# GpSimd's loads ahead of its scalings of v, and VectorE's order of work at the start of group 1, in a block attention with an MLP

## The chip, the cores and the metric

The kernel runs on one core of a Trainium2 chip. The metric is the device time of one execution in microseconds (us). Engines are named as the profile names them: PE is TensorE (PEld its weight loads), DVE is VectorE, ACT is ScalarE, POOL is GpSimd, SP is the queue that issues most stores and the DMA transposes.

## What is computed

Two stages follow each other. A linear attention with decay over blocks (4 batches, 8 heads, 768 positions, head size 64), then an MLP with an exact gelu on the 3072 tokens of 512 values:

```
for b in range(nb):
    intra = einsum('bhic,bhjc->bhij', qb, kb) * Dmask
    intra = einsum('bhij,bhjd->bhid', intra, vb)
    inter = einsum('bhid,bhde->bhie', qb * lam_pow, kv_state)
    out[:, :, sl] = intra + inter
    kv_state = lam_block * kv_state + einsum('bhsd,bhse->bhde', kb * rev_pow, vb)
x = out as (3072, 512);  h = x @ w_in (512 x 2048);  g = gelu(h);  result = g @ w_out (2048 x 512)
```

## The kernel before

**Tiling.** The work is cut into 24 chunks of 128 positions of one batch, and six groups of four chunks (M = 4, one chunk of each batch). Chunks 0 to 3 are group 0, chunks 4 to 7 group 1, chunks 8 to 11 group 2. The attention of one group's chunks is computed while the MLP of the group before runs on TensorE, so that TensorE always has matmuls. All work is in bfloat16 with sums in float32 in PSUM.

**A chunk.** Its k, q and v are loaded by GpSimd's DMA queue (`load`, L69 for the chunks touched here, L72 in halves for later ones), into 10 buffers for k and 8 each for q and v. v is scaled by powers of lambda (`decay_v`, L160, 128x512, on GpSimd; that of chunk 4 alone on VectorE). k and q are transposed on TensorE (L166) with the copies on ScalarE and VectorE (L169, L172), or from chunk 8 on by DMA transposes on SP (L181, L182). The scores are matmuls (L200), masked by VectorE (`masked`, L206: two operations a chunk, each out of one PSUM bank). The answers add what the states give (L248) and what the values give (L255); they are emptied into the group's x by ScalarE (L347), by VectorE for chunk 7 (L345). The states of the next group are made from products of k and scaled v (`next_products`, L215), an addition by VectorE (`added`, L234, called by `sums`) and a scaling by VectorE (`next_states`, L240, called by `new_states`).

**The MLP of a group.** Group 0 does the first product plainly (L666, with the gelu at L669). From group 1 on, part of the first product (L428) and the whole second product (L542) are done as seven products of half-sized blocks in place of eight. That takes sums of blocks: four sums of parts of w_in, once (`w_in_sums`, L389), four sums of x in each group (`x_sums`, L404), sums of w_out (L370) and of g (L521). The seven products gather in PSUM banks that ScalarE copies (L434) and VectorE adds up (`total`, L437). In the second product VectorE makes the last additions into the output tile (`upper`, L621; `lower`, L633) and SP stores it (L553). Of the seven first products of a group, the fifth needs the first sum of x and of w_in, the sixth the second ones, the third the fourth sum of w_in, the seventh the third ones, the fourth the fourth sum of x.

**The order.** It is written by hand: each engine does its instructions in the order in which the program issues them, and waits with semaphores for the others. The program walks over blocks of matmuls; before each block it issues what is due. In group 0 that is listed by block (`group0`, blocks counted from e = 19); from group 1 on a step is put at a place g + f, where B is the length of one plain block of 8 matmuls, so `1 + 4.5 * B` is four and a half blocks into group 1. The steps of group 1 that count here are `visit_at(1 + 1 * B, ...)`, which asks for the scores of chunks 6 and 7 and masks them, and `visit_at(1 + 4 * B, ...)`, which gives their answers and makes the products for the states. The sums of x are issued ahead of the blocks at 4 B (first two) and 4.5 B (last two). The scalings of v of chunks 8 to 11 come at 7 B, on GpSimd, behind a small copy that waits for the fourth sum of x (`behind_sums`, L889). PSUM has eight banks under the names sc, mh, mo (two each), t and o; the next user of a name waits until the last one is emptied.

**GpSimd's order around the change.** Loads of chunks 4 to 7, then for n = 5, 6, 7 the scaling of v of chunk n and the loads of chunk n + 3, then the loads of chunk 11. Each load takes GpSimd's time (L69), whether or not the data has landed.

Of the kernel before, what the change touches and what calls it, by code (L numbers as in the profile page):

```python
# [15 lines left out]
def kernel(  # L16
# [10 lines left out]
    nc = tc.nc  # L27

    B, H, S, D = q.shape
# [10 lines left out]
    M = 4  # L40
# [21 lines left out]
    def chunk_of(name, n):  # L62
        so, b = n // M, n % M
        return dram[name][b, :, so * C:(so + 1) * C, :].rearrange("h si d -> si h d")

    def load(n, name):
        raw[n, name] = qkv_pool.tile([128, H, D], BF16, tag=name, name=f"{name}_t", bufs=10 if name == "k" else 8)
        if name == "v" or n < N_UP:
            nc.gpsimd.dma_start(raw[n, name], chunk_of(name, n))  # L69
        else:  # L70
            for r in range(2):
                nc.gpsimd.dma_start(raw[n, name][:, r::2, :], chunk_of(name, n)[:, r * HP:(r + 1) * HP, :])  # L72
# [78 lines left out]
    def begin(n, early=False):  # L151
        c = Chunk()
        c.n, c.sb, c.early = n, n // M, early
        c.q, c.k, c.v = (raw.pop((n, name)) for name in "qkv")
        return c

    def decay_v(c, eng):

        c.v_dec = work_pool.tile([128, H, D], BF16, tag="vd", name="v_dec", bufs=6)
        eng.tensor_mul(c.v_dec, c.v, lam_m[:, :, None].to_broadcast((128, H, D)))  # L160
# [13 lines left out]
    def transposes(c, tags="mh mh"):  # L174
        for name, tag, empty in zip("kq", tags.split(), (nc.scalar.copy, scaled)):
            transposed(c, name, tag, empty)
# [205 lines left out]
    def w_in_sums(*which):  # L382
        lo, hi = (w_in_t[:, :, (k0 + KW[0]) * 128:(k0 + KW[0] + NW) * 128] for k0 in (0, KH))
        for i in which:
            w_in_s[i] = w_pool.tile([128, 2, NW * 128], BF16, name=f"wi_sum{i}")
            a, b, op = {1: lambda: (hi[:, :2], hi[:, 2:], ALU.add), 2: lambda: (w_in_s[1], lo[:, :2], ALU.subtract),
                        3: lambda: (lo[:, :2], hi[:, :2], ALU.subtract),
                        4: lambda: (lo[:, 2:], w_in_s[2], ALU.subtract)}[i]()
            nc.vector.tensor_tensor(w_in_s[i], a, b, op=op)  # L389
# [3 lines left out]
    def first_blocks(g, g_t, x_t, mm1):  # L393
# [105 lines left out]
        plan += [(his[2], plain), (y.p7, plain // 2), (his[3], plain), (y.p4, plain // 2)]  # L499
        return plan  # L500

    def blocks_by_seven(g, g_t, first):

        last = g == NG - 1
# [31 lines left out]
        banks, sb = {}, {}  # L536
# [13 lines left out]
        def store(rows, us, cols, queue=nc.sync):  # L550
            b = slice(rows * 2 + us.start, rows * 2 + us.stop)
            dst = out_r[g, :, b, cols]
            queue.dma_start(dst, sb[rows][:, us, cols])  # L553

        both, every = slice(0, 2), slice(0, d_model)

        def chain(i, name, u, begin=False):
            if begin and u == 0 and name == "a" and apart:
                banks["a"] = [bank([128, DH], F32, tag, "a_ps") for tag in ("mo", "t" if last else "mo")]
            elif begin and u == 0:  # L560
                all_us = bank([128, 2, DH], F32, "mo" if name == "a" else "mh", f"{name}_ps")
                banks[name], banks[name, "all"] = [all_us[:, 0, :], all_us[:, 1, :]], all_us
            product(i, u, banks[name][u], begin and (u == 0 or (apart and name == "a")))

        def per_bank(name, u, f):
            if (name, "all") not in banks:
                f(slice(u, u + 1), banks[name][u][:, None, :])
            elif u == 1:
                f(slice(0, 2), banks[name, "all"])
# [62 lines left out]
        def lower():  # L632
            nc.vector.tensor_add(sb[1][:, :, d_hi], sb["p5"], sb["u3"])  # L633

        def m4(u):
            chain(4, "a", u)
            per_bank("a", u, lambda us, a: nc.scalar.copy(sb[1][:, us, d_lo], a))
            if last:
                store(1, slice(u, u + 1), d_lo, nc.scalar if u else nc.sync)
            elif u == 1:  # L640
                if g == 0:
                    lower()
                store(1, both, every)

        order = ((m1, 0), (m1, 1), (m2, 0), (m2, 1), (m5, 0), (m5, 1), (m6, 0), (m6, 1), (m3, 0), (m7, 0), (m7, 1), (m3, 1),
                 (m4, 0), (m4, 1))
        if g == 0:
            order = [(f, u) for f in (m1, m5, m2, m3, m6, m7, m4) for u in range(2)]
            run, cost = blocks[N1 - 2]
            blocks[N1 - 2] = (lambda: ([g_sum(i, 0) for i in (1, 2, 4, 3)], run())), cost  # L650
# [47 lines left out]
    live = {}  # L698
# [52 lines left out]
    for n in range(M, 2 * M):  # L751
        live[n] = begin(n)
        if n > M:
            decay_v(live[n], nc.gpsimd)
            for name in "kqv":
                load(n + M - 1, name)
    for name in "kqv":
        load(3 * M - 1, name)
    next_load[0] = 3 * M
# [15 lines left out]
    def triangles():  # L775
        for p in HALVES:
# [20 lines left out]
        e + 11: [lambda: visit([], [4]), lambda: masks(4)],  # L797
        e + 12: [lambda: scores_by_quarters(live[5], "t o"), lambda: masks(5), lambda: transposes(live[6])],
        e + 13: [lambda: visit([4, 5], []), lambda: empties(4, 5), lambda: transposes(live[7], "mo mh"),
                 lambda: w_in_sums(1, 2)],  # L800
    }

    todo = []
# [1 line left out]
    def at(when, run):  # L805
        todo.append((place(when), run))

    def begin_at(when, n):
        def run():
            live[n] = begin(n)  # L810
            dma_transposes(live[n])
        at(when, run)
# [3 lines left out]
    def visit(done, asked, banks="mo mo", states_of=(), kv_tags="mh mh"):  # L816
        done = [live[n] for n in done]
        if done:
            o_ps = [bank([128, HP, C], F32, tag, "o_ps") for tag in ("o", "t")]
            from_states(done, o_ps, 0)  # L820
        for n, tags in zip(asked, ("sc sc", banks)):
            scores_by_quarters(live[n], tags)
        if done:
            if not asked:
                apart = bank([128, HP, C], F32, "sc", "apart_ps")
                for p in HALVES[::-1]:
                    nc.tensor.matmul(apart[p, 0, :], idle[p, :D], idle[p, :C], start=True, stop=True,
                                     skip_group_check=True)
            from_states(done, o_ps, 1)
            for n, tag in zip(states_of, kv_tags.split()):  # L830
                totals[n] = next_products(n, tag)
            for c, c.o_ps in zip(done, o_ps):
                from_values(c)
        for n in asked:
            prefetch(n + M)
# [21 lines left out]
    def empties(*chunks):  # L857
        for n in chunks:
            empty_outputs(live[n])
# [14 lines left out]
    def visit_at(when, done, asked, *then, **how):  # L874
        at(when, lambda: visit(done, asked, **how))
        for step in then:
            w, run = when, step[0]
            if isinstance(run, float):
                w, step = run, step[1:]
            at(w, lambda step=step: step[0](*step[1:]))  # L880

    B = 2 * M * 2 * C / later
# [27 lines left out]
    for i, w in enumerate((-0.07, 0.0, 0.13)):  # L910
        begin_at(1 + w, 2 * M + i)
    at(1 + 7 * B, lambda: prefetch(3 * M))
    begin_at(1 + 7 * B, 2 * M + 3)
    visit_at(1 + 1 * B, [], [2 * M - 2, 2 * M - 1], (masks, 2 * M - 1, 2 * M - 2),
             (w_in_sums, 4, 3), banks="t o")
    visit_at(1 + 4 * B, [2 * M - 2, 2 * M - 1], [], (empties, 2 * M - 2, 2 * M - 1), (sums, M, M + 2),
             (1 + 4.5 * B, new_states, M), (1 + 4.5 * B, new_states, M + 2), states_of=(M, M + 2), kv_tags="sc sc")
    n = 2 * M
    steps((1 + 7 * B, behind_sums, 1), (1 + 7 * B, decays, *range(n, n + M)),
          (1 + 7 * B, prefetch, 3 * M + 1), (1 + 11 * B, prefetch, 3 * M + 2),  # L920
# [9 lines left out]
    for g in range(2, NG):  # L930
        n = (g + 1) * M
# [27 lines left out]
    for g in range(1, NG - 2):  # L959
        n = (g + 2) * M  # L960
# [48 lines left out]
```

## Time and profile before

| | us |
|---|---|
| median of 3 runs | 198.13 |
| lowest and highest run | 197.66, 198.58 |
| the profiled execution | 198.04 |
| its span, from first to last instruction | 196.0 |
| PE busy in it | 187.9 (96%) |
| DVE busy | 135.2 (69%) |
| POOL busy | 112.1 (57%) |
| ACT busy | 106.3 (54%) |
| granted TensorE clock | 1.0 of full speed all through |

The profile is of one execution. Its timeline gives for each entry the start in us from the span's beginning, the busy time, the engine, the line of the program, the operation, what it writes and reads, the count, and in brackets the engine's idle time just before with what ended it. Entries that follow each other closely on one line are merged (x2, x4). Neighbours on an engine can overlap a little, as instructions are pipelined; the distance from start to start tells more than the busy time. The chain that ended last is followed back from the last instruction, at each step to what released it. Group 0's MLP ends at about 49.6 us, group 1's first product lies between 49.6 and 67 us.

### The profile page before, as it was taken

How to read it: one execution, taken by the hardware profiler on the slowest of the kernel's cores; microseconds unless marked ns; L12 is line 12 of the kernel's file. 1: busy time of each engine (PE TensorE's matmuls, PEld its weight loads, DVE VectorE, ACT ScalarE, POOL GpSimd, SP SyncE). 2: the span in 40 equal slices, each digit the busy share in tenths (PEclk: the TensorE clock that was granted, in tenths of full speed). 3: DMA queues.
4: the chain of work that ended last, by engine and by line, in shares of the span. 5: the costliest groups of instructions: out<-in, count | busy, mean ns of one | idle time of the engine just before them, and what ended most of it. 6: DMA issues, size and time to landing. Idle time of an engine off the chain costs nothing.

```text
span 196.0 us, 6742 instructions
## 1 busy us (share of the span) xinstructions
PE 187.9 (96%) x2932; PEld 160.4 (82%) x2932; DVE 135.2 (69%) x231; ACT 106.3 (54%) x210; POOL 112.1 (57%) x141
## 2 busy tenths in 40 slices
PE   7699999998999999999999999999999999999992
PEld 3278776997878898888999888999888888888881
DVE  3744509997998699597797398687459693545830
ACT  4954566144548812659932279712379522589231
POOL 8999992699997599998099756980040000000000
PEclk9999999999999999999999999999999999999999
DMA  4999999999999999999979999999600000400005
GB/s 115 146 170 176 195 197 197 165 157 220 155 215 124 159 123 146 137 144 285 135 47 126 103 201 242 83 89 123 244 2 3 0 3 27 190 3 0 0 3 214
DMA packets 104781, 24.82 MB, mean 127 GB/s; under 512 B 93232, under 2 KB 101936, under 8 KB 104752
## 3 DMA queue, kind: packets, MB, share of 16 engines
q0 software_dynamic: 83120, 13.38, 108.9%
q1 hardware_dynamic: 21488, 10.89, 28.4%
q8 instruction: 23, 0.38, 0.8%
q10 hardware_dynamic: 144, 0.13, 0.2%
q14 instruction: 6, 0.05, 0.1%
HBM read 27.27 MB, written 6.29 MB: 171 GB/s over the span
## 4 chain that ended last, share of the span: by engine, by line
PE 85%; DVE 7%; DMA 3%; POOL 2%; issue 1%; ACT 0%; POOLq 0%; DVEq 0%
PE h_ps L666 24%; PE a_ps L542 19%; PE c_ps L542 11%; PE ha_ps L428 9%; PE b_ps L542 5%; PE hc_ps L428 5%; DMA q_t<-in_q_dram 3%; DVE sc_m L206 2%; PE hb_ps L428 2%; PE o_ps L314 2%; PE o_ps L255 1%; PE kv_ps L290 1%; PE o_ps L326 1%; PE t_ps L166 1%; PE idle_ps L707 1%; PE sc_ps L279 1%
## 5 line engine op out<-in xcount | busy, mean ns | idle before, releaser
L666 PE MATMUL h_ps<-x_t,w_in_t 128*128 128x256 bf16 (+3 forms) x480 | 55.7, 266 | 0.2 <-DVE x_t L345 0.2
L666 PEld LDWEIGHTS <-w_in_t 128*128 128x128 bf16 x480 | 41.7, 98 | 7.4 <-DVE x_t L345 0.5
L669 ACT ACTIVATE g_t<-h_ps 128x512 bf16<-128x512 f32 (+2 forms) x59 | 34.1, 578 | 23.6 <-PE h_ps L666 23.6
L542 PEld LDWEIGHTS <-g_sum 128*128 128x128 bf16 x456 | 38.3, 98 | 3.6
L542 PEld LDWEIGHTS <-g_t 128*128 128x128 bf16 x360 | 29.3, 98 | 2.7
L160 POOL TENSOR_TENSOR v_dec<-v_t,lam_m 128x512 bf16<-128x512 bf16 x23 | 24.0, 1065 | 10.1 <-PE a_ps L542 5.4
L69 POOL DMA_DIRECT2D v_t<-in_v_dram x24 | 22.0, 915 | 4.2 <-DMA w_out_t<-in_moe_w_out_dram 1.8
L542 PE MATMUL a_ps<-w_sum,g_sum 128*128 128x256 bf16 (+1 forms) x240 | 23.2, 251 | 0.0
L521 DVE TENSOR_TENSOR g_sum<-g_t 128x1024 bf16<-128x1024 bf16 x24 | 16.0, 699 | 9.6 <-ACT g_t L669 9.6
L72 POOL DMA_DIRECT2D k_t<-in_k_dram x24 | 18.5, 791 | 0.0
L72 POOL DMA_DIRECT2D q_t<-in_q_dram x24 | 18.3, 790 | 0.0
L428 PEld LDWEIGHTS <-wi_sum 128*128 128x128 bf16 x160 | 15.6, 97 | 2.5 <-issue 0.2
L574 ACT COPY f_u<-a_ps 128x256 f32<-128x256 f32 (+1 forms) x16 | 7.7, 479 | 17.7 <-PE a_ps L542 17.7
L333 DVE TENSOR_TENSOR x_t<-o_ps,lam_q 128x512 bf16<-128x512 f32 x16 | 10.3, 684 | 4.2 <-PE o_ps L314 4.2
L440 ACT ACTIVATE g_t<-h_p 128x512 bf16<-128x512 f32 x20 | 12.9, 644 | 0.4 <-DVE h_p L437 0.3
L428 PEld LDWEIGHTS <-w_in_t 128*128 128x128 bf16 x120 | 11.6, 98 | 1.8
L69 POOL DMA_DIRECT2D k_t<-in_k_dram x12 | 11.1, 925 | 2.3 <-DMA w_out_t<-in_moe_w_out_dram 2.1
L542 PE MATMUL c_ps<-w_out_t,g_sum 128*128 128x256 bf16 (+1 forms) x112 | 12.3, 257 | 0.0
L428 PE MATMUL ha_ps<-x_sum,wi_sum 128*128 128x256 bf16 x80 | 12.0, 272 | 0.0
L437 DVE TENSOR_TENSOR h_u<-h_u,hc_ps 128x512 f32<-128x512 f32 x10 | 6.8, 684 | 7.3 <-ACT h_u L434 5.3
L69 POOL DMA_DIRECT2D q_t<-in_q_dram x12 | 10.9, 906 | 1.4 <-DMA w_out_t<-in_moe_w_out_dram 1.4
L542 PE MATMUL c_ps<-w_sum,g_sum 128*128 128x256 bf16 (+1 forms) x104 | 11.7, 265 | 0.0
(109 smaller groups left out, 326.4 us busy)
## 6 DMA issues: line engine op xcount, KB each, us to landing
out_dram<-o_sb SPq DMA_DIRECT2D x11, 512.0 KB, 5.1
v_t<-in_v_dram POOLq DMA_DIRECT2D x24, 128.0 KB, 6.4
w_out_t<-in_moe_w_out_dram POOLq DMA_DIRECT2D x4, 512.0 KB, 8.7
w_in_t<-in_moe_w_in_dram POOLq DMA_DIRECT2D x7, 256.0 KB, 7.6
k_t<-in_k_dram POOLq DMA_DIRECT2D x12, 128.0 KB, 6.6
q_t<-in_q_dram POOLq DMA_DIRECT2D x12, 128.0 KB, 5.9
k_t<-in_k_dram POOLq DMA_DIRECT2D x24, 64.0 KB, 5.3
q_t<-in_q_dram POOLq DMA_DIRECT2D x24, 64.0 KB, 5.1
```

Of the source, the lines that this page charges most:

```text
L69: nc.gpsimd.dma_start(raw[n, name], chunk_of(name, n))
L72: nc.gpsimd.dma_start(raw[n, name][:, r::2, :], chunk_of(name, n)[:, r * HP:(r + 1) * HP, :])
L160: eng.tensor_mul(c.v_dec, c.v, lam_m[:, :, None].to_broadcast((128, H, D)))
L333: nc.vector.tensor_mul(x[:, :, :, HALVES[t]], pairs[n].o_ps[t], lam_q[:, :, None, HALVES[t]].to_broadcast((128, HP, 2, D)))
L428: nc.tensor.matmul(self.banks[b][:, k, :], left[i](q, self.kf + k), right[i](q), start=(tag is not None and k == 0 and q == 0), stop=(q == 1),
L437: nc.vector.tensor_add(self.sb[name], self.sb[name], self.banks[b])
L440: nc.scalar.activation(g_t[:, k0 + self.kf:k0 + self.kf + 2, cols], src, ACT.Gelu)
L521: nc.vector.tensor_tensor(gsum[i][:, ks, :], part(a), part(b), op=op)
L542: nc.tensor.matmul(o[:, d], left[i](k, slice(u * C, (u + 1) * C)), right[i](k)[:, d], start=(begin and k == 0 and d.start == 0), stop=(k = ...
L574: per_bank(src, u, lambda us, src: nc.scalar.copy(sb[name][:, us, :], src))
L666: nc.tensor.matmul(h_ps[:, k, :], w_in_t[:, ki, (kf + k) * 128:(kf + k + 1) * 128], x_t[:, ki, cols], start=(k == 0 and ki == 0), stop=(ki ...
L669: nc.scalar.activation(g_t[:, kf:kf + ks, cols], h_ps, ACT.Gelu)
```

## The change

Three things are moved; nothing is added to the arithmetic and nothing taken away.

1. On GpSimd, the loads of chunks 8, 9 and 10 are each issued ahead of the scaling of v of chunk 5, 6 and 7 that they followed.
2. The last addition of group 0's output (`lower`, L633) and the store behind it are held until the masks of chunks 7 and 6 in group 1 are issued. Of the four sums of w_in, only the first stays at the end of group 0; the second and fourth go to 2 B and the third to 4.5 B in group 1 (before: the second at the end of group 0, the fourth and third behind the masks).
3. The additions for the states (L234) go from 4 B to 5.5 B, behind the sums of x, and the scalings of the states (L240) from 4.5 B to 10 B.

```diff
+    held = []
+
+    def finish_held():
+        while held:
+            held.pop(0)()
...
+            elif u == 1 and g == 0:
+                held.extend([lower, lambda: store(1, both, every)])
             elif u == 1:
-                if g == 0:
-                    lower()
                 store(1, both, every)
...
     for n in range(M, 2 * M):
         live[n] = begin(n)
         if n > M:
-            decay_v(live[n], nc.gpsimd)
             for name in "kqv":
                 load(n + M - 1, name)
+            decay_v(live[n], nc.gpsimd)
...
-                 lambda: w_in_sums(1, 2)],
+                 lambda: w_in_sums(1)],
...
-    visit_at(1 + 1 * B, [], [2 * M - 2, 2 * M - 1], (masks, 2 * M - 1, 2 * M - 2),
-             (w_in_sums, 4, 3), banks="t o")
-    visit_at(1 + 4 * B, [2 * M - 2, 2 * M - 1], [], (empties, 2 * M - 2, 2 * M - 1), (sums, M, M + 2),
-             (1 + 4.5 * B, new_states, M), (1 + 4.5 * B, new_states, M + 2), states_of=(M, M + 2), kv_tags="sc sc")
+    visit_at(1 + 1 * B, [], [2 * M - 2, 2 * M - 1], (masks, 2 * M - 1, 2 * M - 2), (finish_held,),
+             (1 + 2 * B, w_in_sums, 2, 4), banks="t o")
+    visit_at(1 + 4 * B, [2 * M - 2, 2 * M - 1], [], (empties, 2 * M - 2, 2 * M - 1), (1 + 4.5 * B, w_in_sums, 3),
+             (1 + 5.5 * B, sums, M, M + 2), (1 + 10 * B, new_states, M, M + 2), states_of=(M, M + 2), kv_tags="sc sc")
```

## Prediction, made before the changed kernel was run

> **What bounds the kernel now.** I read four views in this order: the chain that ended last (by engine), TensorE's waits, the timelines of the engines between 37 and 68 us, and VectorE's operations against GpSimd's in the same microseconds.
>
> ```profile
> PE 85%; DVE 7%; DMA 3%; POOL 2%; issue 1%; ACT 0%; POOLq 0%; DVEq 0%
> ...
> 42.01 1.45 DVE v_dec L160
> 43.47 0.60 DVE o_sb L621
> 44.06 0.60 DVE qT L172
> 44.66 2.40 DVE sc_m L206 x4
> 47.11 0.41 PE o_ps L248 x8
> ```
>
> The first line is the page's chain by engine, the others are the chain in order of time (start, length). TensorE carries the end for 85% of the span. After the start-up the only long stretch on another engine is VectorE's, from 40.7 to 47.1 us. The view of TensorE's waits names none after 58.5 us. So from there on, a microsecond won before 58.5 us is won at the end, unless something new stops TensorE. TensorE's own timeline shows the places (start, busy, idle before and releaser):
>
> ```profile
> 44.72 0.42 PE L200 MATMUL sc_ps<-qT,kT 64*64 64x128 bf16 x16 [0.18 <-DVE qT L172]
> ...
> 47.11 0.41 PE L248 MATMUL o_ps<-qT,state 64*64 64x128 bf16 x8 [0.55 <-DVE sc_m L206]
> ...
> 56.58 1.05 PE L666 MATMUL h_ps<-x_t,w_in_t 128*128 128x256 bf16 x8 [0.24 <-DVE x_t L345]
> ```
>
> Matmul ends are modelled, so I count lost time from start to start. Eight 128x256 matmuls take 0.87 us in the undisturbed rows; the ones at 45.52 lead to 47.11, so 0.72 us are lost there.
>
> Why VectorE is late at 47.1 stands in two pairs of rows, VectorE's and GpSimd's:
>
> ```profile
> 41.93 1.53 DVE L160 TENSOR_TENSOR v_dec<-v_t,lam_m 128x512 bf16<-128x512 bf16 x1
> ...
> 49.56 1.30 DVE L389 TENSOR_TENSOR wi_sum<-w_in_t 128x1024 bf16<-128x1024 bf16 x1
> 50.90 0.69 DVE L389 TENSOR_TENSOR wi_sum<-wi_sum,w_in_t 128x1024 bf16<-128x1024 bf16 x1
> ```
>
> ```profile
> 41.64 1.28 POOL L160 TENSOR_TENSOR v_dec<-v_t,lam_m 128x512 bf16<-128x512 bf16 x1 [0.47 <-DMA v_t<-in_v_dram]
> ...
> 49.25 1.06 POOL L160 TENSOR_TENSOR v_dec<-v_t,lam_m 128x512 bf16<-128x512 bf16 x1
> ```
>
> The same kind of sum takes 1.30 us beside GpSimd's scaling and 0.69 without it. Both long VectorE rows end 0.55 us after the scaling on GpSimd (42.92 to 43.47, 50.31 to 50.87). VectorE does nothing of such an operation until GpSimd is through. VectorE rows with one input in PSUM (L437 beside the scalings at 61 to 63 us) stay at 0.68; loads issued by GpSimd beside VectorE's sums stretch neither.
>
> The Trainium skill ("SBUF — State Buffer", "Who interferes with whom") says the same as a rule: a VectorE operation with two SBUF inputs and a GpSimd operation that reads SBUF exclude each other for a whole instruction. The trace agrees (0.55 us behind the end, twice).
>
> **Part 1: GpSimd's loads of chunks 8 to 11 ahead of the scalings.** Nothing is added or removed: 12 loads of 0.88 to 0.93 us and three scalings of 1.06 change places. Now the order is scaling 5, load 8, scaling 6, load 9, scaling 7, loads 10, 11. Afterwards load 8 starts when chunk 7's last load ends (41.13), the 0.47 us wait for v of chunk 5 vanishes, and with 2.69 us for three loads the scalings run at 43.8 to 44.9, 47.5 to 48.6 and 51.2 to 52.3, two us later than now. Their users: values of chunk 5 at 47.7, state products of chunks 6 and 7 at 54.6; with TensorE moved up as below they want them at 46.9 and 53.6. The cover is 2.0 and 1.3 us. What VectorE does at the new times has a PSUM input (L621, L172, L206), or VectorE is idle. So v_dec of chunk 4 falls from 1.53 to 0.69 us, the length of L172 and L240 rows of the same 128x512 shape: **0.84 us**. Bounds: 0 (if 1.53 is its own length) and 0.93 (0.60, the pitch from start to start of such rows, L206's).
> The VectorE chain runs without a gap from there to the masks that end at 47.06, so they end at 46.21 and L248 starts at 46.26. TensorE alone would be there at 46.03 to 46.13, so all 0.85 us count; the two waits of 0.18 and 0.55 shrink to about 0.15.
> The first w_in sum comes at 48.7, behind scaling 6 (ends 48.6), and falls to 0.69 as well. The DMA transposes on SP are used from 66.4 us on; now chunk 9's wait behind the store issued at 52.27, afterwards ahead of it. Chunk 11's land near 70 us and are wanted at 71.9, 71 afterwards: covered.
>
> **Part 2: masks ahead of w_in sums and of the held addition.** L633 (0.60) and the second w_in sum (0.61) leave the place ahead of the masks of chunks 7 and 6, the first one is 0.6 shorter. These masks start now at 52.11 behind VectorE's queue; afterwards at 50.4, when their scores are there (51.24 now, less 0.85). State products (L215) start now at 54.65 where their forerunners (54.20, 0.25 for eight) would let them at 54.45: **0.2 us** won. Behind the masks VectorE does L633 and two w_in sums, 1.8 us from 52.8 to 54.7, and the copy of chunk 7 (L345) is wanted at 54.76: covered by 0.1 us, no more. The wait of 0.24 at L666 stays, since that copy follows TensorE's own values.
> The store leaves SP some 2.7 us later; the tile it reads is written again only at 74 us and later.
>
> **Part 3: sums of x ahead of the steps for states.** Two additions (L234, 1.20) and, by ten blocks, two scalings of states (L240, 1.20) go behind the x sums; one w_in sum (0.60) comes between. The fifth product (L428, hc) now starts at 58.10, 0.64 after its forerunner where 0.44 is usual, since the x sum ends at 58.05; afterwards that is ready at 55.8 against 56.8: **0.2 us** won. L437 then starts at 58.7 (60.30 now), 1.6 earlier, against TensorE's 1.25. ScalarE works without a gap from 61.01, released by that L437, and three starts on TensorE (61.63, 62.17, 63.17) come 0.04, 0.10 and 0.13 late behind buffers that L437 and ScalarE empty: **0.25 us** won.
> Against it stands a new collision. The state scalings (both inputs in SBUF) move from 58.42 to about 61.3, into GpSimd's scalings of chunks 8 to 11:
>
> ```profile
> 59.93 0.89 POOL L69 DMA_DIRECT2D v_t<-in_v_dram  x1 [1.40 <-DMA v_t<-in_v_dram]
> ...
> 60.95 3.05 POOL L160 TENSOR_TENSOR v_dec<-v_t,lam_m 128x512 bf16<-128x512 bf16 x3
> ...
> 65.12 0.69 DVE L437 TENSOR_TENSOR h_p<-h_p,ha_ps 128x512 f32<-128x512 f32 x1 [0.55 <-PE ha_ps L428]
> ...
> 65.86 0.60 PE L428 MATMUL ha_ps<-x_sum,w_in_t 128*128 128x256 bf16 x4
> ```
>
> Behind the state scalings stand two L437; the second reads the bank that TensorE writes next (65.81 against 65.86 now, wanted at 64.36 afterwards). Undisturbed the pair ends in time. Each of the two can wait for the rest of one GpSimd scaling. Worked through by the start of the first: 60.4 gives 0.4 us of new wait on TensorE, 60.95 (as now) 0.95, 61.6 gives 0.4, after 62 none; the worst is 1.2. That start hangs on when v of chunk 10 lands (59.4 now). Its queue is never empty from 44 to 59 us, so earlier issues alone don't pull it in, while the store's later place in DMA can shift it either way by about 1 us. I take **0.6 us** lost, about the mean of these; ends 0 and 1.2.
>
> **Sum.** 0.85 + 0.2 + 0.2 + 0.25 - 0.6 = 0.9 us. The profiled execution took 198.04 us (span 196.0, 2.0 around it), 0.09 under the median of 198.13. 198.04 - 0.9 = **197.1 us**.
>
> **Rivals.**
> - *No collision.* GpSimd's scalings start after 62, or the state scalings fall beside loads. For it: v of chunk 10 has DMA traffic ahead of it that moves. Against it: 60.95 lies in the middle of the danger. 198.04 - 1.5 = 196.5.
> - *The 1.53 us is v_dec's own length.* For it: it is the one such row on VectorE. Against it: the w_in sum with the same 0.55 behind the scaling. Then 0.65 - 0.6: 198.0, and the change does nothing.
> - *Loads ahead delay the scalings.* GpSimd waits at loads for landings (1.77 at 31.47, 1.40 at 59.93). If it does so for 2 us among loads 8 to 10, scaling 7 misses L215's 1.3 us of cover by 0.7: 197.8. Against it: the loads of 42.9 to 55.5 have no wait at all now.
> - *Slower: VectorE starved.* If GpSimd's back-to-back scalings don't let VectorE in between, both state scalings wait for the third one's end at 64.0; the second L437 then ends at 66.35 and TensorE waits 2.0 us instead of 0.6: 198.04 - 1.5 + 2.0 = 198.6, 198.9 if the run of three starts at 61.25. It decides from a loss of 1.5 us on. Against it: at 97.64 a GpSimd scaling got in between two back-to-back VectorE sums after 0.13 us (1.19 for 1.06), so the waiting one came first.
>
> The Trainium skill (same page, "SBUF: two separate sides") has the rule that whichever starts first holds the ports for its instruction and the other blocks fully. It does not say who comes first of one that waits and one that follows, so by it both 197.1 and 198.6 can come; no row here shows VectorE waiting before two GpSimd scalings in a row.
>
> **Chances.** Forecast 0.50 (its own range 196.8 to 197.6), no collision 0.24, own length 0.08, late scalings 0.10, starved 0.08. The range 196.3 to 198.1 leaves out the starved case and some scatter (the three runs differ by 0.9). A measurement tells about 0.5% (1 us) from no change, so faster means under 197.1: all of "no collision" and a little over half of the forecast, 0.52. Slower means over 199.1: what little of the starved case scatters that far up, and what I don't see, 0.06. The rest, 0.42, is within.
>
> **What would show it.** Right: v_dec on VectorE near 0.69, first w_in sum 0.69, L248 at 46.3, L215 at 53.6, the hc product 0.44 after its forerunner, and one or two L240 rows over 1 us near 61.3 with a TensorE wait for L437 near 64.4. Wrong: v_dec still near 1.5; a TensorE wait on v_dec near 53; L240 rows at 0.68 (no collision) or the first at over 2.5 us (starved).

## The result, and the profile after

| | before | after |
|---|---|---|
| median of 22 runs each, us | 197.89 | 197.21 |
| lowest and highest | 196.68, 198.79 | 196.35, 198.00 |
| the profiled execution | 198.04 | 197.59 |
| its span | 196.0 | 195.8 |

The ratio of after to before is 0.9967, 95% interval 0.9951 to 0.9982: 0.7 us faster, clear of zero and under the 0.5% that a single measurement tells. The forecast was 197.1 us and 0.9 us. That the total came so near is partly chance: the forecast started from 198.04, and the 22 runs of before have a median of 197.89.

The chain that ended last, by engine, for the profile after:

```profile
PE 71%; POOL 12%; DVE 8%; DMA 7%; issue 1%; ACT 0%; POOLq 0%; DVEq 0%
```

TensorE has not become less important: it is 96% busy as before. In this execution the chain is followed from VectorE's w_out sums at 37 us back into the landing of w_out, in place of TensorE's early work. These sums wait for that landing, and VectorE's row of work up to L248 hangs on it. So executions are best compared from the last w_out sums on: the last row of two, which starts at 40.73 in the profile before and at 40.59 after. VectorE's timeline of before has it, and the state scalings as they were:

```profile
40.73 1.28 DVE L370 TENSOR_TENSOR w_sum<-w_out_t,w_sum 128x1024 bf16<-128x1024 bf16 x2
...
58.42 1.29 DVE L240 TENSOR_TENSOR state<-tmp,lam_c 128x512 bf16<-128x512 f32 x2
```

VectorE's timeline of after (start, busy, engine, line):

```profile
40.59 1.29 DVE L370 TENSOR_TENSOR w_sum<-w_out_t,w_sum 128x1024 bf16<-128x1024 bf16 x2
41.79 0.69 DVE L160 TENSOR_TENSOR v_dec<-v_t,lam_m 128x512 bf16<-128x512 bf16 x1
...
48.58 0.98 DVE L389 TENSOR_TENSOR wi_sum<-w_in_t 128x1024 bf16<-128x1024 bf16 x1
...
61.25 2.98 DVE L240 TENSOR_TENSOR state<-tmp,lam_c 128x512 bf16<-128x512 f32 x2
64.16 0.68 DVE L437 TENSOR_TENSOR h_u<-h_u,hc_ps 128x512 f32<-128x512 f32 x1
64.76 0.68 DVE L437 TENSOR_TENSOR h_p<-h_p,ha_ps 128x512 f32<-128x512 f32 x1
```

GpSimd's:

```profile
44.20 1.12 POOL L160 TENSOR_TENSOR v_dec<-v_t,lam_m 128x512 bf16<-128x512 bf16 x1
...
60.04 3.04 POOL L160 TENSOR_TENSOR v_dec<-v_t,lam_m 128x512 bf16<-128x512 bf16 x3
```

TensorE's, with the idle time before and its releaser:

```profile
46.12 0.41 PE L248 MATMUL o_ps<-qT,state 64*64 64x128 bf16 x8 [0.43 <-DVE sc_m L206]
...
55.46 1.05 PE L672 MATMUL h_ps<-x_t,w_in_t 128*128 128x256 bf16 x8 [0.25 <-DVE x_t L345]
...
65.49 0.60 PE L428 MATMUL ha_ps<-x_sum,w_in_t 128*128 128x256 bf16 x4 [1.05 <-DVE h_p L437]
```

The scaling of v of chunk 4 takes 0.69 us, now that GpSimd scales at 44.2 instead of at 41.6. L248 starts 5.53 us behind the start of the last w_out sums, 6.38 before: 0.85 us won. But the two state scalings, 1.20 us from the start of the first to the start of what followed them before, now hold VectorE from 61.25 to 64.24 beside GpSimd's three scalings. The second L437 is late, and TensorE waits 1.05 us for it, a wait that was not there. Laid against before matmul by matmul, TensorE gains 0.85 us up to L248 (counted from the w_out sums), 0.13 at L215, 0.20 at the fifth product, 0.20 at the starts behind ScalarE; it loses 1.15 at 65.49 and 0.20 within the scores of chunk 11 (72 us).

Profiles of three further executions of the changed kernel agree up to 63 us. They lose less at 65: 0.48, 0.21 and 0.38 us; and 0.3, 0.42 and 0.48 near 72. The first profile is the unlucky one at 65 us. None of the four stands for the middle of the runs: they took 197.43 to 197.67 us, above the median of 197.21, and in the three further ones the w_out sums start 0.3 to 0.4 us later than before.

### The profile page after: what moved, and what is told of

Its sections match the earlier page's. It is cut to its first block, busy times and chain, and to the rows that moved or that the text cites. A ratio compares the mean times of both kernels' runs of the same rounds, so it can differ in the third digit from the quotient of the medians.

```text
span 195.8 us, 6743 instructions
## 1 busy us (share of the span) xinstructions
PE 187.6 (96%) x2932; PEld 160.2 (82%) x2932; DVE 135.4 (69%) x231; ACT 106.3 (54%) x210; POOL 111.8 (57%) x141
## 4 chain that ended last, share of the span: by engine, by line
PE 71%; POOL 12%; DVE 8%; DMA 7%; issue 1%; ACT 0%; POOLq 0%; DVEq 0%
PE a_ps L548 18%; PE h_ps L672 16%; PE c_ps L548 9%; PE ha_ps L428 9%; DMA w_out_t<-in_moe_w_out_dram 7%; PE hc_ps L428 5%; PE b_ps L548 4%; POOL w_in_t L94 3%; DVE sc_m L206 2%; PE hb_ps L428 2%; POOL v_dec L160 2%; PE o_ps L314 2%; POOL k_t L69 2%; POOL q_t L69 2%; POOL v_t L69 2%; DVE w_sum L370 1%
## 5 line engine op out<-in xcount | busy, mean ns | idle before, releaser
L672 PE MATMUL h_ps<-x_t,w_in_t 128*128 128x256 bf16 (+3 forms) x480 | 55.7, 266 | 0.4 <-DVE x_t L345 0.2
L672 PEld LDWEIGHTS <-w_in_t 128*128 128x128 bf16 x480 | 41.6, 98 | 7.9 <-DVE x_t L345 0.5
L548 PEld LDWEIGHTS <-g_sum 128*128 128x128 bf16 x456 | 38.2, 98 | 3.7
L548 PEld LDWEIGHTS <-g_t 128*128 128x128 bf16 x360 | 29.3, 98 | 2.7
L548 PE MATMUL a_ps<-w_sum,g_sum 128*128 128x256 bf16 (+1 forms) x240 | 23.2, 251 | 0.0
L548 PE MATMUL c_ps<-w_out_t,g_sum 128*128 128x256 bf16 (+1 forms) x112 | 12.3, 257 | 0.0
L548 PE MATMUL c_ps<-w_sum,g_sum 128*128 128x256 bf16 (+1 forms) x104 | 11.7, 265 | 0.0
L580 ACT COPY f_p<-c_ps 128x512 f32<-128x512 f32 x6 | 3.5, 586 | 15.0 <-PE c_ps L548 15.0
```

The source lines that it names most:

```text
L548: nc.tensor.matmul(o[:, d], left[i](k, slice(u * C, (u + 1) * C)), right[i](k)[:, d], start=(begin and k == 0 and d.start == 0), stop=(k = ...
L580: per_bank(src, u, lambda us, src: nc.scalar.copy(sb[name][:, us, :], src))
L672: nc.tensor.matmul(h_ps[:, k, :], w_in_t[:, ki, (kf + k) * 128:(kf + k + 1) * 128], x_t[:, ki, cols], start=(k == 0 and ki == 0), stop=(ki ...
```

## The experiments

Ratios are to the kernel before, timed beside each version on the same chip. L666, L542 and L553 of before are L672, L548 and L559 in the changed kernel, and one less in the two with the store late.

**Part 1 alone.** The kernel before, with only GpSimd's order changed:

```diff
-            decay_v(live[n], nc.gpsimd)
             for name in "kqv":
                 load(n + M - 1, name)
+            decay_v(live[n], nc.gpsimd)
```

> Part 1 alone: only GpSimd's loads of chunks 8 to 10 go ahead of the scalings, VectorE's order is that of before. Ports theory (VectorE can't work on two SBUF inputs while GpSimd scales): v_dec of chunk 4 takes 0.69 us in place of 1.53, L248 starts 0.85 us earlier relative to the w_out sums, the first w_in sum is 0.7 to 1.0, the masks of chunks 7 and 6 start when their scores are there, no collision at 61 us since the state scalings (L240) stay at 57 to 59 us with 0.68 each. Time 0.9 to 1.1 us under before (ratio 0.9945 to 0.9955): better than the whole change. Landing theory (what helped is that k, q and v of chunks 8 to 11 are there sooner): the first use of these is at 66 us on TensorE, so nothing moves before that, and TensorE had no wait there: ratio 1.000.

Measured: ratio 0.9970 (0.9944 to 0.9997). VectorE's timeline:

```profile
42.05 0.69 DVE L160 TENSOR_TENSOR v_dec<-v_t,lam_m 128x512 bf16<-128x512 bf16 x1
...
57.58 1.29 DVE L240 TENSOR_TENSOR state<-tmp,lam_c 128x512 bf16<-128x512 f32 x2
```

L248 stands 5.54 us behind the last w_out sum (6.38 before) although VectorE's order is that of before, so GpSimd's order alone makes the 0.85 us, long before any of the earlier loads is used; the landing theory falls. The state scalings are undisturbed (0.68 each) and TensorE waits nowhere for L437. The interval takes in 0.9945 to 0.9955 as well as 0.997: the size stays loose, the place is clear. L215 starts 0.13 us earlier here too, with VectorE's old order. In time this version can't be told from the whole change (0.9967), and at the product behind chunk 11's scores (73 us) it is 0.68 us ahead of before, counted from the w_out sums: as far as these runs tell, part 1 alone makes the gain.

**Parts 2 and 3 alone.** The changed kernel, with GpSimd's order put back.

> Parts 2 and 3 without part 1: GpSimd's order is that of before, VectorE's that of after. Ports theory: v_dec of chunk 4 stays at 1.5 us and L248 waits as before; the parts win 0.2 (L215) + 0.2 (fifth product) + 0.25 (L437 and ScalarE) = 0.65 us, and the state scalings collide with GpSimd's three scalings at about 61 to 64 us, where the first takes 1.5 to 3 us and TensorE waits 1 to 2 us for the second L437 behind them. Net 0.35 to 1.35 us slower than before, ratio 1.002 to 1.007. If the reordering of VectorE were itself the gain, the ratio would be about that of the whole change, 0.997.

Measured: 0.9985 (0.9964 to 1.0006). VectorE's timeline:

```profile
41.95 1.53 DVE L160 TENSOR_TENSOR v_dec<-v_t,lam_m 128x512 bf16<-128x512 bf16 x1
49.58 1.29 DVE L389 TENSOR_TENSOR wi_sum<-w_in_t 128x1024 bf16<-128x1024 bf16 x1
...
62.26 1.94 DVE L240 TENSOR_TENSOR state<-tmp,lam_c 128x512 bf16<-128x512 f32 x2
```

The long rows are back (1.53 and 1.29), and L248 is 6.38 us behind the w_out sum. The 0.13, 0.20 and 0.20 us are won as in the whole change. The expectation of a slower kernel failed: with VectorE 1.0 us later the state scalings start at 62.26, beside the last of GpSimd's three scalings only (60.00 to 63.04), and the second L437 ends at 65.40, just as TensorE wants it; that cost 0.1 us. Nearly all that was left of the 0.54 us won by then went at 72 us: TensorE lost 0.5 us around the scores of chunk 11, and the product behind them starts 0.14 us later than before, counted from the w_out sums. GpSimd's run began 0.9 us earlier than before (60.00 against 60.95) here too, so part 1 is not its cause; the later place of the store in part 2 is the likely one, which was not tried by itself.

**State scalings late.** The whole change, with

```diff
-             ... (1 + 10 * B, new_states, M, M + 2), ...
+             ... (1 + 13.5 * B, new_states, M, M + 2), ...
```

> The whole change, with the two state scalings (L240) put at 13.5 blocks into group 1 in place of 10, behind both L437 that stood behind them. Ports theory: the wait of 1.05 us that TensorE has for L437 at 65.5 us vanishes, the seventh product is followed by the fourth in 2.9 us less 1.15, L240 takes 0.68 each at about 65 us; 1.1 us better than the whole change: ratio to before 0.991 to 0.9925. If the wait at 65.5 us costs nothing because TensorE would stand elsewhere soon after: ratio stays 0.996 to 0.997.

Measured: 0.9944 (0.9923 to 0.9965). TensorE's view of waits names L437 no more; its timeline has a new entry:

```profile
64.65 0.60 PE L428 MATMUL ha_ps<-x_sum,w_in_t 128*128 128x256 bf16 x4
...
71.21 0.48 PE L279 MATMUL sc_ps<-qT,kT 64*64 64x64 bf16 x16 [0.31 <-DMA qT<-q_t]
```

The wait at 65 is gone, but 0.6 to 0.7 us is lost again at 71: the scores of chunk 11 wait for its DMA transposes, which land at 71.17. The gain over before is 1.1 us, under the 1.5 to 1.8 expected.

**Memsets between the scalings.** The whole change with a GpSimd memset (128x64) behind each of the scalings of v of chunks 8 to 11.

> The whole change with a small GpSimd memset (128x64, writes only) behind each of the scalings of v of chunks 8 to 11. In the changed kernel the first state scaling waited to the end of three scalings in a row (2.39 us). If VectorE gets its turn as soon as an operation without SBUF input stands between GpSimd's scalings, the first L240 row is 1.4 us or less and the second waits for one scaling of its own (1.0 to 1.6 us); TensorE's wait at 65.5 stays about 1 us, as the pair ends at about the same time. If the queue is held for all of GpSimd's run, the first row is 2.5 us or more.

Measured: 196.87 us in one execution. It did not answer its question. GpSimd's run began at 58.90, so the first L240 (61.44) met the last scaling (61.08 to 62.15) and ended 0.56 us behind it; the second was free (0.68), and TensorE waited nowhere for L437.

**Store late.** State scalings late, and the held store not beside its addition but at 8 B (`finish_held` now does one of its two steps each time):

```diff
+    steps((1 + 8 * B, finish_held), (1 + 7 * B, behind_sums, 1), ...
```

> The whole change with the state scalings at 13.5 blocks, and with group 0's last store issued at 8 blocks, behind the DMA transposes of chunk 11 (the addition that it waits for stays where the change put it). With the state scalings late alone, TensorE's order had a new wait at 71.2 us: the scores of chunk 11 waited 0.6 us for its transposes, landed at 71.2. Transfer theory: the 512 KB of the store take DMA time from the loads of chunk 11 (landed 61.0 and 64.1); with the store behind them they land 1 us or more earlier, the transposes land before 70.3, the wait at 71.2 goes, ratio to before 0.990 to 0.993. Rival (the transposes themselves or the number of loads in flight set the time, not the store): the transposes land at 70.8 or later, ratio 0.994 as with the state scalings late alone.

Measured: 0.9945 (0.9925 to 0.9965). SP's timeline with the state scalings late, where the last line is the q transpose of chunk 11:

```profile
54.85 0.54 SPq L559 DMA_DIRECT2D out_dram<-o_sb  x1
...
61.04 1.20 SPq L181 DMA_TRANSPOSE kT<-k_t  x1
64.08 1.19 SPq L182 DMA_TRANSPOSE qT<-q_t  x1
```

and with the store late:

```profile
60.30 1.19 SPq L181 DMA_TRANSPOSE kT<-k_t  x1
62.48 1.19 SPq L182 DMA_TRANSPOSE qT<-q_t  x1
63.77 0.52 SPq L558 DMA_DIRECT2D out_dram<-o_sb  x1
```

That transpose starts 1.6 us earlier, although this execution's w_out sums are 0.7 us later, and lands at 69.14 instead of 71.17. So the transfer theory holds for the landing, while the ratio is the one expected of its rival (0.994): the time is no better. The state scalings at 65.20 met GpSimd's scaling of chunk 11 (64.86 to 65.90), and the sums of g behind them made TensorE wait 0.24 us at 70.9. One wait that is taken away uncovers the next.

**Scalings done twice, in a row.** The whole change with GpSimd doing each of these four scalings twice.

> The whole change with each scaling of v of chunks 8 to 11 done twice by GpSimd (same result, 8 operations, of which at least six follow each other without a pause from about 60 us on). If VectorE doesn't get its turn between GpSimd's scalings that follow each other, the first state scaling (L240 at about 61.3) lasts until the end of the whole run of at least six, 4.5 to 6 us, and TensorE waits 3 us or more at the fourth product. If it does get its turn, the first L240 takes 1.6 us or less, and the second again about 1.6.

Measured: 197.72 us in one execution. The first L240 took 1.04 us, the second 1.53: VectorE got its turn after the scaling that ran, and GpSimd's next one waited (1.49 for 1.04). TensorE lost 0.65 us at the fourth product. One doubt: a pause of 0.08 us stood ahead of each doubled scaling, so not every pair followed without a gap.

**The same with memsets between.**

> The same eight scalings on GpSimd with a small memset (128x64, writes only) behind each. If a memset gives VectorE its turn, the first L240 waits for one scaling at the most (1.6 us or less) and the second for one more; TensorE's wait at the fourth product is 1 to 2 us. If GpSimd's queue is kept as long as scalings wait in it, L240 lasts 4.5 us or more, as without the memsets.

Measured: 199.26 us in one execution; its w_out sums came 1.1 us later than in the profile of before, so the total says little. L240 took 1.24 and 1.53 us, each until 0.55 behind one scaling. As without the memsets: they change nothing that these rows show.

**Scalings behind the states.** The whole change, with GpSimd's copy ahead of the scalings of chunks 8 to 11 reading the second new state, and loads of chunk 13 behind them:

```diff
-    steps((1 + 7 * B, behind_sums, 1), (1 + 7 * B, decays, *range(n, n + M)),
-          (1 + 7 * B, prefetch, 3 * M + 1), ...
+    steps((1 + 10 * B, behind_states, n + 2), (1 + 10 * B, decays, *range(n, n + M)),
+          (1 + 10 * B, prefetch, 3 * M + 1), ...
```

> The whole change, with GpSimd's scalings of v of chunks 8 to 11 held until the second state scaling is done (the small copy ahead of them reads that state in place of the fourth sum of x), and the loads of chunk 13 behind them; VectorE's order is that of the change. Ports theory: both L240 rows take 0.68 at 61.3 and 61.9, no TensorE wait for L437 near 65; the scalings run at about 62.5 to 66.7, in time for the products at 65. What is left is the wait for chunk 11's transposes near 71 (0.5 us). Ratio to before 0.993 to 0.9955. Queue theory (L437 is late because two operations of 0.6 stand before it, whatever GpSimd does): the wait near 65 stays at 0.5 us or more, ratio 0.996 to 0.998.

Measured: 0.9966 (0.9942 to 0.9991). VectorE's timeline, in the order of the changed kernel:

```profile
61.37 1.29 DVE L240 TENSOR_TENSOR state<-tmp,lam_c 128x512 bf16<-128x512 f32 x2
62.58 0.68 DVE L437 TENSOR_TENSOR h_u<-h_u,hc_ps 128x512 f32<-128x512 f32 x1
63.72 0.69 DVE L437 TENSOR_TENSOR h_p<-h_p,ha_ps 128x512 f32<-128x512 f32 x1 [0.46 <-PE ha_ps L428]
```

With GpSimd out of the way the same two operations at the same place take 1.2 us, L437 waits for TensorE and not the other way round. So the queue theory falls by these rows, and the wait at 65 is GpSimd's. The ratio alone would not have told: 0.9966 lies in the range expected of the queue theory. What was won went, to 0.6 us, into the wait for chunk 11's transposes (0.31 idle at 71.12, on TensorE).

**Both moved.** The same, and the store behind the transposes of chunk 11.

> The same, with group 0's last store issued behind the transposes of chunk 11 as well (8 blocks). With both waits gone the 1.5 us won before 65 us remain but for 0.2 to 0.4 us that TensorE waits for the sums of g near 71: ratio to before 0.9925 to 0.995, and no worse than the state scalings late with the store late, 0.9945.

Measured: 196.58 us, ratio 0.9917 (0.9888 to 0.9946): 1.4 us faster than before by the medians, 1.6 by the ratio, a little more than expected. It is the lowest ratio here, though its interval overlaps several others, that of the state scalings late (0.9923 to 0.9965) among them. In the view of TensorE's waits from 42 to 90 us one line is left:

```profile
PE h_ps L671 <- DVE x_t L345: 0.2, 1, 0.2
```

Chunk 11's transposes land at 67.66, 2.6 us ahead of their use.

**The changed kernel again, three times.**

> The changed kernel once more. In its profile the state scaling was passed over by one of GpSimd's scalings that stood in line (2.39 us), where a doubled run of scalings later let it in after one (1.04 and 1.53). If passing over is the rule for plain scalings in a row, the first L240 again ends 0.55 us behind the last scaling of the run in which it started, when it started before the last one. If it depends on the moment, or on where the scalings lie, the row is another one: 0.7 to 1.6 us. Ratio to before about 0.997.

> The changed kernel a third time, for its first L240 row alone. Two profiles gave 2.39 us (started 0.21 us behind the start of the middle scaling, and the last scaling passed it) and 0.88 us (started 0.77 us behind it, and went ahead of the last). If the later of two waiters always loses, and GpSimd's next scaling counts as waiting from early in the one before: a start early in a scaling that is not the last gives its rest plus a whole scaling plus 0.55 us, a start late in it the same; so 0.88 stays the exception. If VectorE goes first whenever it waits: rest plus 0.55 us, and 2.39 stays the exception.

> The changed kernel a fourth time, with the same two readings: the first L240 is the rest of the scaling that runs plus 0.55 us, or a whole scaling (1.0 us) longer. TensorE's wait for L437 near 65.4 goes with the end of the second L240: none if that is by 62.5, 1.05 if by 64.2.

Measured: ratio 0.9955 (0.9929 to 0.9982) for the second; single executions of 197.55 and 197.67 us for the others. VectorE's and GpSimd's rows of the second:

```profile
61.75 2.33 DVE L240 TENSOR_TENSOR state<-tmp,lam_c 128x512 bf16<-128x512 f32 x2
```

```profile
59.97 3.55 POOL L160 TENSOR_TENSOR v_dec<-v_t,lam_m 128x512 bf16<-128x512 bf16 x3
```

Here GpSimd's run is 0.5 us longer: its last scaling waited for the first L240 (0.88 us), then the second L240 waited for that scaling (1.52). In the third the first L240 started 0.15 us into the last scaling and took 1.45. In the fourth it started 0.06 us before the middle scaling's end, and the last one, begun 0.02 us later, went first: 1.61. So a waiting VectorE was passed over in two profiles (the first and the fourth) and went ahead in one; in the doubled runs it went ahead each time. Which comes first is not settled by these rows.

## Why the prediction was right, and where it was not

**The gain in part 1** (0.84 at v_dec, 0.85 at L248) came out exactly: 0.69 us for the scaling in every profile with part 1, 5.53 to 5.54 us from the w_out sum to L248 in place of 6.38. Part 1 alone, and parts 2 and 3 without it, show both sides. The rival "1.53 is its own length" is out. TensorE's wait at L248 was to shrink to about 0.15 us: it is still 0.43 and 0.5 in the first two profiles of the changed kernel, and none is named in the other two.

**The w_in sum** was to be 0.69 too; it took 0.98, and 1.25, 0.72 and 0.72 in the other three executions. Scaling 6 ended at 48.97 in place of 48.6, 0.39 us behind the sum's start; in the second it ended 0.70 behind it, in the last two ahead of it. Nothing came of it: VectorE then waits 0.47 to 0.99 us for scores.

**Part 2 and the fifth product**: 0.2 + 0.2 forecast, 0.13 + 0.20 measured. The 0.13 is not part 2's alone: part 1 alone has it as well, and the two don't add up. The copy of chunk 7, covered by 0.1 us only, was in time: L345 keeps its wait of 0.25.

**L437 and ScalarE**: 0.25 forecast, 0.20 measured.

**The collision** was forecast at its place, with its victim (the second L437) and a cost of 0.6 us (0 to 1.2). Four profiles show 1.15, 0.48, 0.21 and 0.38, a mean of 0.56. That this meets 0.6 is partly luck: the runs of scalings began before 60.4, the earliest start that the prediction worked through (0.4 us there), and in two profiles VectorE was passed over, which the prediction held for a rival and the term did not count. That GpSimd's run depends on when v of chunk 10 lands was right (the load ahead of the run starts 0.53 us behind that landing, before and in three of the four profiles of the changed kernel); that it moves was right (from 60.95 to between 59.55 and 60.04). It moved with parts 2 and 3 alone as well (60.00), and little with part 1 alone (60.73), so the earlier loads are not the cause, as forecast.

**The starved rival** was half right: VectorE was passed over in two profiles. But the run had come forward by about a microsecond, so even then its end at 63.08 cost 1.15 and not 2.0 us. I had reckoned it with the run at 60.95.

**The step that failed** is the cover of chunk 11's transposes: "land near 70 us and are wanted at 71.9". SP's timeline of before has the q transpose:

```profile
63.57 1.23 SPq L182 DMA_TRANSPOSE qT<-q_t  x1
```

It lands at 71.39 (the last update of its semaphore in the trace), so the cover was 0.5 us and not two. In after it starts at 64.89 and lands at 71.55, 0.06 ahead of the first matmul that wants it. Counted from the w_out sums it starts at 20.6 and 20.9 us in the two versions with the store behind it, and at 22.4 to 24.5 in the twelve other profiles, where the store is ahead of it. The sum had no term for it. Of the 1.4 us won by 65 us, state scalings late loses 0.7 there and scalings behind the states 0.6; with both moved, TensorE's waits name the transposes no more.

**What stays open.** In the profiles of the changed kernel TensorE loses 0.2 to 0.5 us within the scores of chunk 11; the trace names no engine for it (in two of them it says "issue"). The transposes land close to these scores, but that they cause the loss here is not shown; in the kernels with the states or the scalings moved the trace names the transposes. In both moved, where these land long before, 0.16 us are still lost there. The rest is not explained. Nor is the rule by which VectorE or GpSimd goes first.

Why the whole is 0.7 and not 0.9: the measured terms are 0.85 + 0.13 + 0.20 + 0.20 = 1.38 in the first profile (1.34 to 1.37 in the others), less 0.56 for the collision and about 0.4 near 72 (0.35 within the scores, the rest before the next product), a loss that the forecast did not have. That leaves some 0.4 us for these four executions. The medians say 0.7, with an interval of 0.4 to 1.0. So the mechanism of part 1 was right, the nearness of the whole to 0.9 owes something to luck, and parts 2 and 3 win 0.4 us by 63 us that the collision and the scores of chunk 11 take back.

## What to carry to other kernels

When an operation on VectorE takes about twice its usual time, look at what GpSimd does in the same microseconds, and move the one that has slack. When an operation with two SBUF inputs is moved, look up what GpSimd does at the new place, in several executions, since GpSimd's times hang on landings. And where an end is won earlier, look up the landing of each transfer in the trace; a cover that is only estimated may be a quarter as long.

## What the runs showed of the hardware

- VectorE's operation with two SBUF inputs ends about 0.55 us (0.545 to 0.560) behind the GpSimd scaling that held it, in 26 rows of these profiles between 38 and 72 us, with bf16 and with float32 inputs. Seven w_in sums that began in the last 0.07 to 0.39 us of a scaling end 0.59 to 0.81 us behind it; why is open. GpSimd waits in the same way (1.49 and 1.54 us for 1.04).
- A waiting operation is not always served first when the other engine has the next one in line: VectorE was passed over in two of three plain runs of scalings, and in none of four rows of the doubled ones.
- With a 512 KB store issued 9 us later, the transpose behind a load of 128 KB started 1.6 us earlier and landed 2.0 us earlier: the place of a store on SP bears on the landing of loads on GpSimd's queue.
